# A mixer block on one NeuronCore: all of x and w2 first, w3 and w4 issued by ScalarE behind early gelus, layer 1 nearly in one piece, its later tiles turned by DMA

## The chip, the cores and the metric

The kernel runs on one core of a Trainium2 chip. The metric is the device time of one execution in microseconds (us). Several executions of each kernel are taken in rounds beside the kernel before on the same chip; the profiled execution is one of them. A run counts as slow when it is over 1.5% above the fastest of its kernel.

## The reference

```python
B, S, D, F = 1, 2048, 512, 1792          # bf16
def reference(x, w1, w2, w3, w4):
    h = gelu(layernorm(x) @ w1)          # layer 1
    # four quarters of h's columns are shifted along S by +1, -1, +2, -2 (zeros come in)
    x1 = x + shifted(h) @ w2             # "mixing"
    return x1 + gelu(layernorm(x1) @ w3) @ w4   # "up2" and "down"
```

S is cut into 16 tiles of 128 rows. A normalized tile must be transposed ("turned") before it can enter a product. A turn is made either by TensorE (four 128x128 matmuls against the identity into PSUM, then a copy by ScalarE or DVE) or by a DMA transpose from SBUF to SBUF, issued by SyncE.

## The kernel before

The program is a list of operations with what they read and write. TensorE's order is written out in SCRIPT; loads are listed in LOADS, and an operation goes to SyncE's queue unless "@act" sends it to ScalarE's. The order on the other engines is found by a list scheduler with fixed costs. "tyN" or "tpN" in SCRIPT turns tile N on TensorE (N over 15 means tile N-16 of layer 2), "up1:g" is layer 1's product of group g, "mix:t" the mixing of tile t, "up2:g" and "down:t" are layer 2. Every tile not turned in SCRIPT is turned by DMA:

```python
GROUPS = {1: (1, 1, 1, 1, 2, 1, 4, 2, 2, 1), 2: (2, 4, 4, 2, 4)}     # tiles in a group
LOADS = """
x1 x2 tp2 x0@act w1a w1b x3 x4-5 tp5 w2a w2b x6-7 w3 tp17 w4a x8-10 w4b tp6 x11-12 tp1 tp16 x13-15
"""
SCRIPT = """
warm:9 sa:0 sb:0 ty:1 ra:0 rb:0 ty:2 up1:1 th:0 up1:2 mix:0 ty:3 ty:5 mix:1 ty:4 up1:3-4 ty:16 mix:2 ty:17
mix:3 up2:0 mix:4 up1:5 down:1 down:0 mix:5 up1:6-7 mix:8 mix:6 up1:9 mix:9-10 up1:8 mix:7 mix:11 up2:1
...   # (cut)
"""

def load(item):
    name, _, eng = item.partition("@")
    eng = eng or "sp"
    ...   # (cut) one dma_start of whole x tiles, or of a half ("a", "b") or all of a weight

def ln(layer, t):
    ...   # (cut) statistics on DVE or ScalarE, rstd by pow on GpSimd, normalization into xn_buf
    if q not in pe_tp:
        pg.add("sp", f"tp{q}",
               lambda e: e.dma_start(xT[:, :, P * t : P * (t + 1)], xn_buf[:, slot(q), :], transpose=True),
               reads=[(("xn", slot(q), hh), q) for hh in (0, 1)],
               writes=[(("xT", t, c), layer) for c in range(DC)], queue="tp")
```

SyncE's queue carries loads, DMA turns and, later, outputs, in order. Before, w3 and w4 stand in that same queue between loads of x.

## Time and profile before

| what | value |
|---|---|
| time, median of the first three runs | 135.79 us (135.78 to 136.6) |
| time beside the experiments, medians | 135.15 to 135.44 us |
| span of the profiled run | 134.6 us (its time was 135.96 us) |
| layer 2's first product starts | 16.8 us |
| turns on TensorE / by DMA | 9 (one of them of h) / 24 |

The chain of waits, read in order of time, names for every moment what the end of the program was waiting for; as long as it names TensorE alone, nothing can be gained by removing a wait elsewhere. The prediction shows these lines. The DMA turns as the view of the transposed tile lists them, smallest, median and largest time from issue to landing:

```profile
DMA to landing us min/median/max: 2.4/2.5/5.9
```

A turn takes 2.5 us when nothing else moves; the ones that took up to 5.9 us stood behind loads in the same queue.

### The profile page before, as it was taken

The page shows a single profiled execution, that of the slowest core. Times are in us where ns is not written, and L with a number is a line of the kernel's source. Part 1 is how long each engine was busy: PE and PEld are TensorE (multiplying, and loading weights), DVE is VectorE, ACT ScalarE, POOL GpSimd, SP SyncE. Part 2 cuts the span into 40 slices and gives each one's busy share as a digit, 9 for nine tenths or more (in the row PEclk, how much of TensorE's full clock was granted, in tenths as well). Part 3 has the DMA queues.
Part 4 walks back from the last instruction along what each step waited for, and adds up shares of the span by engine and source line. Part 5 has one row for each costly group of instructions (what it writes and reads, how often), then busy time and mean ns, then how long its engine had stood idle before and what let it go on. Part 6 is the DMA issues. An engine that isn't in the chain of part 4 may idle for free.

```text
span 134.6 us, 2001 instructions
## 1 busy us (share of the span) xinstructions
PE 130.9 (97%) x776; PEld 71.5 (53%) x789; DVE 50.8 (38%) x134; ACT 58.4 (43%) x92; POOL 29.7 (22%) x68
## 2 busy tenths in 40 slices
PE   8799999999999999999999999999999999999994
PEld 3287688544656444478544444444444444444464
DVE  2689996856178930070061004232222200012222
ACT  5779349989544275547315554000000155520000
POOL 2444549892102860006010001200000000000000
DMA  5999998445452134100411000211111100001112
GB/s 136 323 345 399 361 304 234 90 81 105 90 115 85 24 75 98 39 0 0 83 39 39 0 0 0 65 52 44 39 39 53 64 0 0 0 5 39 39 39 78
DMA packets 21289, 12.19 MB, mean 91 GB/s; under 512 B 13856, under 2 KB 20768, under 8 KB 21280
## 3 DMA queue, kind: packets, MB, share of 16 engines
q1 hardware_dynamic: 20704, 11.80, 32.7%
q10 hardware_dynamic: 576, 0.26, 0.7%
q8 instruction: 6, 0.10, 0.3%
q14 instruction: 3, 0.02, 0.1%
HBM read 6.82 MB, written 2.10 MB: 66 GB/s over the span
## 4 chain that ended last, share of the span: by engine, by line
PE 93%; DMA 4%; SPq 1%; issue 1%; DVE 0%
PE y_ps L626 46%; PE o_ps L695 36%; PE o_ps L666 10%; DMA w_sb<-in_w_dram 4%; PE y_ps L490 1%; SPq L368 1%; PE y_ps L528 0%; SPq L377 0%; DVE o_sb L703 0%; PE o_ps L594 0%; SPq L857 0%
## 5 line engine op out<-in xcount | busy, mean ns | idle before, releaser
L626 PE MATMUL y_ps<-xnT,w_sb 128*128 128x512 bf16 (+2 forms) x421 | 63.4, 308 | 0.2
L626 PEld LDWEIGHTS y_ps<-xnT,w_sb 128*128 128x128 bf16 x424 | 38.3, 98 | 24.8
L641 ACT ACTIVATE h2T<-y_ps 128x1024 bf16<-128x1024 f32 (+1 forms) x29 | 28.6, 993 | 48.8 <-PE y_ps L626 48.6
L695 PE MATMUL o_ps<-w_sb,h2T 128*128 128x512 bf16 (+3 forms) x247 | 48.6, 355 | 0.3
L695 PEld LDWEIGHTS o_ps<-w_sb,h2T 128*128 128x128 bf16 x252 | 23.5, 98 | 24.7
L703 DVE TENSOR_TENSOR o_sb<-o_ps,x_sb 128x512 bf16<-128x512 f32 (+3 forms) x18 | 11.4, 632 | 47.1 <-PE o_ps L695 47.1
L423 POOL TENSOR_TENSOR rstd<-mv,neghalf 128x1 f32<-128x1 f32 x21 | 11.5, 549 | 23.6 <-DVE mv L418 14.8
L416 DVE BATCH_NORM_STATS2 st<-x_sb 128x6 f32<-128x512 bf16 x21 | 14.1, 678 | 3.4 <-DMA x_sb<-in_x_dram 3.2
L666 PE MATMUL o_ps<-w_sb,hT 128*128 128x512 bf16 x59 | 14.9, 379 | 0.3
L423 POOL TENSOR_TENSOR rstd<-vpe,neghalf 128x1 f32<-128x1 f32 x11 | 6.0, 547 | 29.4 <-DVE vpe L412 29.3
L673 DVE SCALAR_TENSOR_TENSOR x_sb<-o_ps,x_sb 128x512 bf16<-128x512 f32 x5 | 3.4, 686 | 19.2 <-PE o_ps L666 19.2
L641 ACT ACTIVATE hT<-y_ps 128x512 bf16<-128x512 f32 (+1 forms) x10 | 8.1, 807 | 5.5 <-PE y_ps L626 5.3
L677 DVE TENSOR_TENSOR x_sb<-o_ps,x_sb 128x512 bf16<-128x512 f32 x11 | 7.6, 687 | 4.4 <-PE o_ps L666 4.1
L666 PEld LDWEIGHTS o_ps<-w_sb,hT 128*128 128x128 bf16 x64 | 6.0, 98 | 5.7
L457 POOL TENSOR_SCALAR xn_buf<-x_sb,rstd,nmr 128x512 bf16<-128x512 bf16 x11 | 8.4, 765 | 0.8 <-DVE nmr L450 0.4
L400 ACT ACTIVATE junk<-x_sb 128x512 bf16<-128x512 bf16 x11 | 6.9, 624 | 2.2 <-DVE x_sb L673 2.2
L454 ACT ACTIVATE xn_buf<-x_sb,nmr,rstd 128x512 bf16<-128x512 bf16 x8 | 6.3, 806 | 0.6 <-POOL nmr L450 0.6
L445 DVE TENSOR_SCALAR xn_buf<-x_sb,mv,rstd 128x512 bf16<-128x512 bf16 x12 | 5.3, 442 | 2.8 <-POOL rstd L423 2.6
L720 PE MATMUL o_ps<-zeros 128*128 128x512 bf16 x9 | 4.0, 631 | 0.4 <-DVE zeros L347 0.4
L395 ACT ACTIVATE junk<-x_sb 128x512 bf16<-128x512 bf16 x6 | 3.7, 624 | 0.8 <-DMA x_sb<-in_x_dram 0.8
L418 DVE BATCH_NORM_AGGREGATE mv<-st 128x2 f32<-128x9 f32 x21 | 3.8, 189 | 0.3
L450 POOL TENSOR_SCALAR nmr<-mv,rstd 128x1 f32<-128x1 f32 x13 | 3.4, 263 | 0.7
(34 smaller groups left out, 28.6 us busy)
## 6 DMA issues: line engine op xcount, KB each, us to landing
out_dram<-o_sb SPq DMA_DIRECT2D x15, 128.0 KB, 1.7
w_sb<-in_w_dram SPq DMA_DIRECT2D x1, 1792.0 KB, 9.7
w_sb<-in_w_dram SPq DMA_DIRECT2D x2, 896.0 KB, 11.5
w_sb<-in_w_dram SPq DMA_DIRECT2D x4, 256.0 KB, 5.2
x_sb<-in_x_dram SPq DMA_DIRECT2D x3, 256.0 KB, 5.1
x_sb<-in_x_dram SPq DMA_DIRECT2D x2, 384.0 KB, 8.9
x_sb<-in_x_dram SPq DMA_DIRECT2D x3, 128.0 KB, 2.6
xnT<-xn_buf SPq DMA_TRANSPOSE x24, 2.5
```

The source lines that it names most:

```text
L400: (lambda d: (lambda e: e.activation(d, src, ACT_F.Square, accum_out=sums[:, q, 1:2])))(junk[:, b, :]),
L416: pg.add("dve", f"bnst{q}", lambda e: e.bn_stats(st9[:, q, 0:6], src), reads=rs, writes=[(("st", q), 0)], dur=605)
L423: lambda e: e.tensor_tensor(col(rstd), var, neghalf[:], ALU.pow),
L445: lambda e: e.tensor_scalar(dst, src, mv[:, q, 0:1], rstd[:, q : q + 1], ALU.subtract, ALU.mult),
L454: f = lambda e: e.activation(dst, src, ACT_F.Identity, bias=nmr[:, q : q + 1], scale=rstd[:, q : q + 1])
L457: f = lambda e: e.tensor_scalar(dst, src, rstd[:, q : q + 1], nmr[:, q : q + 1], ALU.mult, ALU.add)
L626: ins = e.matmul(y_ps[:, p, W * i : W * (i + 1)], wsb[:, dc, P * fc : P * (fc + 1)], src[:, dc, P * t0 : P * t0 + W], start=(dc == 0), sto ...
L641: (lambda d, s: (lambda e: e.activation(d, s, ACT_F.Gelu_apprx_tanh)))(dst, ysrc),
L666: ins = e.matmul(dst, hT[:, j, c0 : c0 + P], w2_sb[:, j, :], start=(j == 0), stop=(j == DC - 1))
L677: f = lambda e: e.tensor_tensor(x1_sb[:, t, :], dst, x_sb[:, t, :], ALU.add)
L695: ins = e.matmul(dst, h2T[:, fc, P * t : P * (t + 1)], w4_sb[:, fc, cs], start=(fc == 0), stop=(fc == FC - 1))
L703: (lambda d, c: (lambda e: e.tensor_tensor(o_sb[:, oi, c], d, x1_sb[:, t, c], ALU.add)))(dst, cs),
```

## The change

The intent: less work on TensorE, the bounding engine (fewer turns, wider groups in layer 2), w3 and w4 out of the way of x, and layer 1 nearly in one piece. TensorE's script and the assignments of side work were searched anew. The diff, cut (constants of the scheduler's cost model, further assignment tables and a list of small priority offsets are left out):

```diff
+        for a, b in self.gates:            # order on one engine without a semaphore
+            assert named[a].eng == named[b].eng, (a, b)
+            order_only.add((named[a].idx, named[b].idx))
 ...
-GROUPS = {1: (1, 1, 1, 1, 2, 1, 4, 2, 2, 1), 2: (2, 4, 4, 2, 4)}
+GROUPS = {1: (1, 2, 1, 1, 1, 2, 1, 2, 2, 2, 1), 2: (4, 4, 4, 4)}
 ...
 LOADS = """
-x1 x2 tp2 x0@act w1a w1b x3 x4-5 tp5 w2a w2b x6-7 w3 tp17 w4a x8-10 w4b tp6 x11-12 tp1 tp16 x13-15
+x0-1 x2 x3 w1a x5 w1b x4 w3@act>gelu1_3_0 tp4 x6 x7 x8 w2a tp4 w2b x11 x9-10 tp3 x15 x12-13 x14
+w4@act>gelu1_1_0
 """
 SCRIPT = """
-warm:9 sa:0 sb:0 ty:1 ra:0 rb:0 ty:2 up1:1 th:0 up1:2 mix:0 ty:3 ty:5 mix:1 ty:4 up1:3-4 ty:16 mix:2 ty:17
-mix:3 up2:0 mix:4 up1:5 down:1 down:0 mix:5 up1:6-7 mix:8 ...
+warm:10 sa:0 sb:0 ty:2 ty:1 ra:0 rb:0 ty:3 up1:1 ty:5 th:0 up1:2 ty:4 up1:4 mix:0 up1:3 mix:1 mix:4 up1:5
+mix:3 mix:2 up1:6 mix:5-6 up1:7 mix:7 up1:8 mix:9 mix:8 up1:9 mix:11 mix:10 up1:10 mix:13 mix:12 up2:1 ...
 """
 ...
-            eng = eng or "sp"
+            eng = eng.partition(">")[0] or "sp"
```

"w3@act>gelu1_3_0" reads: issue w3 from ScalarE after it has issued the gelu of group 3 (tile 4).

## The prediction

> **What bounds the kernel now.** I read the page's busy times first, then the chain of work that ended last in order of time, then the start of the timeline, then the waits.
>
> ```profile
> PE 130.9 (97%) x776; PEld 71.5 (53%) x789; DVE 50.8 (38%) x134; ACT 58.4 (43%) x92; POOL 29.7 (22%) x68
> PE   8799999999999999999999999999999999999994
> PE 93%; DMA 4%; SPq 1%; issue 1%; DVE 0%
> ```
>
> TensorE is busy in 97% of the span, and the slices show no hole after the first two; the other engines have room on average. A busy TensorE could still be waiting in small pieces, so the chain in order of time decides:
>
> ```profile
> 1.47 5.13 DMA w_sb<-in_w_dram
> 6.61 0.05 issue
> 6.65 0.61 PE y_ps L528 x2
> ...
> 8.60 0.92 PE y_ps L626 x16
> ...
> 16.83 6.11 PE y_ps L626 x56
> ...
> 36.81 1.73 PE o_ps L666 x8
> ...
> 129.36 3.48 PE o_ps L695 x43
> 132.84 0.02 issue
> 132.87 0.26 DVE o_sb L703
> ```
>
> Columns: start, length, what. From 6.65 us, where the second half of tile 0's first product starts, to 132.84 us the chain is TensorE alone, with pieces of 0.05 us of issue. It gives me rates: 128 columns 0.92/16, other pieces 0.89/16, so 0.0556 us; 256 columns 6.11/56 = 0.1091; 512 columns 1.73/8 = 0.2158. By these I count what the program must run after 6.65: 460 matmuls of 512 columns (64 mixing, 16 for the group of four tiles in layer 1, 168 in the three large groups of layer 2, 210 down, 2 of tile 0) are 99.27 us; 174 of 256 columns (48 layer 1, 112 layer 2, 14 tail) 18.98; 80 of 128 columns 4.45; 28 transposes (seven tiles) 1.57; the tail's 160 and 96 columns about 1.6. Sum 125.87. The stretch lasts 126.19. So only 0.3 us of it is waiting: no rearrangement can gain by removing waits after the start. After the last matmul come 1.76 us to the end of the span (134.6 - 132.84), and the time is 1.19 us over the span (135.79 - 134.6).
>
> The start is set by loads:
>
> ```profile
> 5.95 1.31 PE L528 MATMUL y_ps<-w_sb,xnT 128*128 128x512 bf16 x4 [0.74 <-DMA w_sb<-in_w_dram]
> 6.07 3.59 SPq L368 DMA_DIRECT2D x_sb<-in_x_dram  x1
> 6.93 0.70 DVE L416 BATCH_NORM_STATS2 st<-x_sb 128x6 f32<-128x512 bf16 x1 [0.76 <-DMA x_sb<-in_x_dram]
> ```
>
> The first row begins when the first half of w1 lands (5.95); its second pair of matmuls waits for the second half (6.65). The second row is a load of x issued with w3 and w4 queued ahead on SyncE's queue: SyncE was held 3.59 us, where a small load ordinarily takes about 0.45.
>
> **What the Trainium skill says.** "TensorE: Matmul & The Clock Gate", section "Wait — 56ns, not 53.3ns?", gives start to start N / 2.4 GHz plus about 2.5 ns per matmul; the rates above agree (55.6 and 215.8 ns), so wider groups gain only 2.5 ns per matmul saved. "DMA: Bandwidth & Descriptors", section "Issuing engines are not separate DMA queues", says that DMAs of all issuing engines run on the same 16 engines and interleave, and that a second issuer saves only sequencer time. The trace before has one x load on ScalarE beside SyncE's at 0.2 us, neither lengthened, too small to test sharing. "Perfetto Trace Analysis", section "DMA Instruction — HWDGE (DVE, Sync)", says the profiled issue lasts until the descriptors are generated, and that generation can outrun the descriptor buffer; the 3.59 us above agrees with a full buffer. This is the danger in putting 1.8 MB loads on ScalarE. No run here shows yet how SyncE's transposes fare beside another queue's load.
>
> **The change part by part.**
>
> (1) Transposes. Tiles 16 and 17 (layer 2) no longer turn on TensorE, and tiles 1 and 2 both turn before the first product, inside the wait for w1. After the second half of tile 0's product four turns remain (tiles 3, 5, 4 and the turn of tile 0's h) in place of seven: 12 x 0.056 = -0.67 us on the bounding engine.
>
> (2) Groups. Layer 2 goes from 2,4,4,2,4 tiles to four fours: 112 matmuls of 256 columns (12.22) become 56 of 512 (12.08), -0.14 us. Layer 1 splits its group of four into twos: 16 x 0.2158 = 3.45 becomes 32 x 0.1091 = 3.49, +0.04 us. Together -0.10. With (1), TensorE's work after the start falls by about 0.77 us. There is nothing else to take: the columns of the two layers, the mixing and the down product are unchanged.
>
> (3) Load order. Before, x1, x2, x0 and half of w1 (640 KB), then the other half (896 KB in all) come first. After, x0-1, x2, x3 stand before the first half (768 KB at its end) and x5 before the second (1152 KB). Before, the second half landed 0.70 us after the first: 256 KB in 0.70 us, 370 KB per us. So the first half lands about 0.35 later (6.3) and the second 256/370 = 0.7 later (7.35). The start moves by +0.7 us. In that wait the turns of tiles 1 and 2 fit: each needs statistics 0.69, aggregate 0.19, the power on GpSimd 0.55, and a normalization of 0.41 (DVE) or 0.76 (GpSimd), so from x at about 3 us both are ready near 6. The tenth warm matmul lies in the same wait and costs nothing.
>
> (4) Layer 1 runs almost without a break. By the rates, after a start at 7.4 the fifteen other tiles and twelve mixings end at about 34 us, where before up2 and down pieces stretched this to about 80 us. By about 25 us DVE must have done the statistics of ten tiles or so (0.69 + 0.19), nine normalizations (0.41), and five or six residual adds (0.69): 8.8 + 3.7 + 3.8 = 16.3 us in spans, and a little less as they overlap at their ends, of some 18 us available. Before, DVE was busy 4.77 and 4.59 us of 5 in the two windows from 10 to 20 us, so such a density is reached but leaves little.
>
> (5) w3 and w4 on ScalarE, behind the gelu of tile 4, about 15 us. Before, w3 and half of w4 took SyncE 1.52 us together, the other half 1.83 us. I estimate 1.5 to 3.5 us of ScalarE. After that gelu TensorE has two mixings, the product of tiles 6-7, two more mixings and the product of tile 8 before a mixing needs the next gelu: 4 x 0.86 + 1.75 + 0.89 = 6.1 us, less the gelu before (0.6) and the next (1.0). So up to about 4 us is hidden. The weights, 3.67 MB at 0.37 MB/us, need 10 us, arrive near 26 us, and layer 2 starts at 34: not on the path.
>
> (6) Transposes by DMA of tiles 8 to 15 now fly with that load. Before, transposes issued between 16 and 24 us, with loads in the queue, landed after 4.5 to 5.9 us; the median is 2.5. Tile 8 is due at about 19 us, 9-10 at 22, 11-12 at 24. Here a delay of 2 us would reach TensorE in part.
>
> Sum: 135.79 - 0.77 + 0.70 = 135.7 without new waits; I put +0.1 for the middle of (4) to (6), whose likely result is nothing but whose unlikely ones are large: **135.8 us**.
>
> **Rivals.** First, new stalls in layer 1: the load on ScalarE's queue delays SyncE's transposes, or ScalarE is held longer than 4 us by its own issue. For it: 4.5 to 5.9 us landings and the 3.59 us of SyncE above. Against: in the old order these transposes sat behind loads in the same queue, which the new one avoids, and all x is issued before. It would make 137 to 140. Second, the start is not later: the early transfer is limited by latency rather than bytes (the memory rate was only about 150 KB per us between 2.5 and 3.5 us before), so w1 lands as before. The full -0.77 then shows, and 135.0 results. Third, DVE becomes the bound of the dense layer 1: its windows were already 92 to 95% busy. Because it catches up only when TensorE waits, that would cost 0.5 to 2 us, 136.3 to 137.7. Fourth, a gain over 2% would need 2.7 us; with 125 us of columns after the start this would require starting 2 us earlier than now, which the later w1 excludes.
>
> **Range and chances.** The lower end is the work saving with no later start and a tighter stretch: 134.8. The upper end gives the stall rivals 2 us: 137.8. Slower by over 2% (beyond 138.5) needs nearly 3 us of stall; I give it 0.12. Faster by over 2%: 0.01.
>
> **What would show each step.** In the chain after, the first product's second half starts at 7.2 to 7.5 (step 3), TensorE alone follows for about 125.4 us (steps 1, 2), with no DMA or DVE piece. The count of turns on TensorE through y_ps falls from 32 to 24. ScalarE's two weight issues sum to 1.5 to 3.5 us, and the product of layer 2 starts near 34 us. The prediction is wrong if the chain between 15 and 30 us goes through DMA transposes, DVE or ScalarE for more than 1 us, if the start is before 6.9, or if a matmul's rate changes.

## The result

The changed kernel takes 142.85 us (median of 4 runs, 142.26 to 144.81) against 135.78 for the kernel before. The ratio of the fast runs is 1.050 (95% interval 1.041 to 1.059): it is slower, and far outside the predicted range. Ratios in this document are the mean time of one kernel's fast runs over that of the other's of the same rounds, so not quite the ratio of the medians quoted. The four runs had granted TensorE clocks of 0.976 (144.81 and 143.42 us) and 0.988 (142.29 and 142.26 us); the kernel before always showed 1.000. The profiled run was the one of 144.81 us, counted as slow.

The page of the changed kernel (busy times; TensorE's busy slices; its granted clock in the same slices; shares of the chain that ended last):

```profile
PE 135.4 (94%) x742; PEld 69.4 (48%) x742; DVE 48.7 (34%) x139; ACT 58.9 (41%) x91; POOL 27.0 (19%) x59
PE   8799980999999999999999999999999999999992
PEclk9999997589999999999999999999999999999999
PE 84%; DMA 8%; DVE 5%; POOL 0%; issue 0%; DVEq 0%; SPq 0%
```

TensorE's share fell from 97 to 94%, a hole stands in the seventh slice, and right behind it the granted clock falls to half. "Busy" rose from 130.9 to 135.4 us although there is less work, mainly since slow matmuls are busy longer. The chain in order of time (start, length, what) shows where the end was set:

```profile
6.37 1.03 PE y_ps L497 x8
7.41 1.71 PE y_ps L535 x4
...
15.93 9.03 DMA xnT<-xn_buf
24.96 0.05 issue
25.01 1.89 PE y_ps L633 x16
26.89 3.38 PE o_ps L673 x8
30.27 1.75 PE y_ps L633 x16
```

The piece of 9.03 us is the DMA turn of tile 8. It was issued at 15.93 us and landed at 24.96; TensorE had nothing to do for the last 4.07 us of it. TensorE's timeline names the wait in brackets (before the bracket: start, length, what), and the view of the transposed tile shows how late turns landed at most:

```profile
25.01 1.89 PE L633 MATMUL y_ps<-xnT,w_sb 128*128 128x128 bf16 x16 [4.07 <-DMA xnT<-xn_buf]
DMA to landing us min/median/max: 2.4/2.5/11.2
```

Then 16 matmuls of 128 columns took 1.89 us (0.89 before), and 8 of 512 columns 3.38 us (1.73): half clock until about 30 us.

The difference of the two profiled runs, 143.5 - 134.6 = 8.9 us of span, adds up as follows. Tile 0's first product ends at 9.11 us (7.41 + 1.71) in place of 7.26 (6.65 + 0.61): +1.85. The gap: +4.07. Half clock behind it: (1.89 - 0.89) + (3.38 - 1.73) = +2.65. Less work on TensorE: -0.77 by the prediction's count. From the last matmul to the end of the span 2.5 us in place of 1.76: +0.8. Together 8.6; 0.3 us stays unassigned. This profile is the slowest of the four runs. Its first product ran at half rate (four matmuls in 1.71 us), which the profile of e_w4late, a fast run 7.6 us slower than the kernel before, did not share; the gap and the half clock behind it did not need that.

The DMA view of two stretches of the changed kernel shows what the turn was waiting for (q10 is ScalarE's queue, q1 SyncE's; packets, MB, share of the 16 engines' time; then turns issued in the stretch and their median us to landing). First 17 to 20 us:

```profile
q10 hardware_dynamic: 240, 0.86, 90.9%
...
xnT<-xn_buf SPq DMA_TRANSPOSE x3, 9.8
```

Then 24 to 26 us:

```profile
q10 hardware_dynamic: 535, 0.55, 82.8%
q1 hardware_dynamic: 534, 0.13, 31.5%
```

From 17 to 20 us SyncE's queue moved no packet at all (q1 is not listed): 240 rows of w3, 3.5 KB each, went by, while turns that had been issued stood still. From 24 to 26 us, with w4's rows of 1 KB, the two queues moved 535 and 534 packets: one for one. A turn has some 577 packets (13,856 packets under 512 B for 24 turns before), so at 267 per us it needs 2.2 us; alone, turns pass at 500 and more per us (e_bothlate). The Trainium skill, "DMA: Bandwidth & Descriptors", section "Queues, rings and completion order", says that each engine goes round robin between queues packet by packet; the second stretch agrees. The section does not describe the first.

ScalarE itself was not held up: its two weight issues took 0.44 and 0.57 us in the timeline. SyncE was: its issue of the turn at 18.71 us took 3.20 us (median 1.27).

### The profile page after: what moved, and what is told of

The parts are those of the page before. It is cut to its first block, busy times and chain, and to the rows that moved or that the text cites. A ratio compares the mean times of both kernels' runs of the same rounds, so it can differ in the third digit from the quotient of the medians.

```text
span 143.5 us, 1924 instructions
## 1 busy us (share of the span) xinstructions
PE 135.4 (94%) x742; PEld 69.4 (48%) x742; DVE 48.7 (34%) x139; ACT 58.9 (41%) x91; POOL 27.0 (19%) x59
## 4 chain that ended last, share of the span: by engine, by line
PE 84%; DMA 8%; DVE 5%; POOL 0%; issue 0%; DVEq 0%; SPq 0%
PE y_ps L633 41%; PE o_ps L702 34%; PE o_ps L673 8%; DMA xnT<-xn_buf 6%; DMA x_sb<-in_x_dram 2%; DVE st L423 2%; PE y_ps L535 1%; PE y_ps L497 1%; DVE xn_buf L452 1%; DVE mv L425 0%; DVE x_sb L680 0%; POOL rstd L430 0%; DVE xnT L505 0%; DVE nmr L457 0%; DVE o_sb L710 0%
## 5 line engine op out<-in xcount | busy, mean ns | idle before, releaser
L633 PE MATMUL y_ps<-xnT,w_sb 128*128 128x512 bf16 (+2 forms) x384 | 64.7, 328 | 4.1 <-DMA xnT<-xn_buf 4.1
L633 PEld LDWEIGHTS y_ps<-xnT,w_sb 128*128 128x128 bf16 x384 | 35.3, 100 | 33.6 <-DMA xnT<-xn_buf 4.6
L648 ACT ACTIVATE h2T<-y_ps 128x1024 bf16<-128x1024 f32 x28 | 28.7, 1024 | 22.0 <-PE y_ps L633 22.0
L673 PE MATMUL o_ps<-w_sb,hT 128*128 128x512 bf16 x64 | 17.1, 410 | 0.0
L648 ACT ACTIVATE hT<-y_ps 128x1024 bf16<-128x1024 f32 (+1 forms) x10 | 8.0, 812 | 9.4 <-PE y_ps L633 9.4
L464 POOL TENSOR_SCALAR xn_buf<-x_sb,rstd,nmr 128x512 bf16<-128x512 bf16 x9 | 6.9, 772 | 8.5 <-DVE nmr L457 7.8
L684 DVE TENSOR_TENSOR x_sb<-o_ps,x_sb 128x512 bf16<-128x512 f32 x9 | 6.2, 689 | 6.3 <-PE o_ps L673 6.1
L452 DVE TENSOR_SCALAR xn_buf<-x_sb,mv,rstd 128x512 bf16<-128x512 bf16 x15 | 6.9, 462 | 1.0 <-POOL rstd L430 0.8
L680 DVE SCALAR_TENSOR_TENSOR x_sb<-o_ps,x_sb 128x512 bf16<-128x512 f32 x7 | 4.8, 684 | 6.1 <-PE o_ps L673 6.1
L497 PE MATMUL y_ps<-ident,xn_buf 128*128 128x128 bf16 x24 | 3.1, 281 | 1.1 <-DVE xn_buf L452 1.1
```

Of the source, the lines that this page charges most:

```text
L452: lambda e: e.tensor_scalar(dst, src, mv[:, q, 0:1], rstd[:, q : q + 1], ALU.subtract, ALU.mult),
L464: f = lambda e: e.tensor_scalar(dst, src, rstd[:, q : q + 1], nmr[:, q : q + 1], ALU.mult, ALU.add)
L633: ins = e.matmul(y_ps[:, p, W * i : W * (i + 1)], wsb[:, dc, P * fc : P * (fc + 1)], src[:, dc, P * t0 : P * t0 + W], start=(dc == 0), sto ...
L648: (lambda d, s: (lambda e: e.activation(d, s, ACT_F.Gelu_apprx_tanh)))(dst, ysrc),
L673: ins = e.matmul(dst, hT[:, j, c0 : c0 + P], w2_sb[:, j, :], start=(j == 0), stop=(j == DC - 1))
L684: f = lambda e: e.tensor_tensor(x1_sb[:, t, :], dst, x_sb[:, t, :], ALU.add)
```

## The experiments

Fourteen kernels ran. In all but four (e_turn8, e_turn6, e_turn6rows, e_pieces) every other instruction kept the changed kernel's order on its engine; but for e_swap this was done by moving finished operations in the list after the scheduler had run. "move(a, b)" puts a right behind b; "fill" puts matmuls on zeros into TensorE's order.

**e_swap: which weight comes first**

```diff
-... x4 w3@act>gelu1_3_0 ...
-w4@act>gelu1_1_0
+... x4 w4@act>gelu1_3_0 ...
+w3@act>gelu1_1_0
```

> Changed kernel with w4 issued first on ScalarE and w3 second; all other instructions in the changed kernel's order. In the changed kernel SyncE's queue moved no transpose packets from 17 to 20 us and then one packet for each packet of the weight queue (250 against 250 per us beside w4's 1 KB rows). Theory A, sharing by packet behind a batch already fetched: w4's rows are 3.5 times smaller, so the batch passes in about 1 us, transposes then move 250 packets per us, tile 8's lands near 20 us, the gap falls from 4.1 to under 1 us and the time to 137.5 to 139.5. Theory B, descriptor generation: SyncE's transposes get no descriptors while ScalarE's two loads are being written, in either order: still no packets for 3 us or more, gap 3 us or more, time 141.5 to 144.5.

Measured: 144.96 us (143.65 to 148.01), ratio 1.072. Theory A missed: between 16 and 19 us only 15 packets of SyncE's queue moved beside 925 rows of w4. After that it was one for one in each us (285 against 281 from 21 to 22, 109 against 107 from 24 to 25 with w3). So the shut-out (the time in which turns get next to no packets) of about 3 us does not depend on which weight is first; in rows it was about 60 per engine here and about 20 in the changed kernel, in bytes about 1 MB both times. The time lies near theory B's figure, but the next run speaks against B's reason. Three of the four runs had 0.988 and 143.65 us, 0.976 and 146.03, 0.965 and 148.01, which looks as if the time went with the granted clock; the fourth, 0.976 and 143.89, does not fit.

**e_w4late: only w3 at the old place**

```diff
+        move("dma_w4", "gelu2_1_0")
```

> Changed kernel with only w4's issue moved later on ScalarE, behind the second gelu of the first group of layer 2; w3 stays where it was. Theory B (generation): w3's 512 rows fit into the buffer, so SyncE's transposes get descriptors at once; packets of both queues run from 17 us on, one for one at about 100 per us while w3 runs, tile 8's 576 packets need 5.5 us, it lands near 22.5, the gap is 1 to 2 us, later tiles go at full rate after 22; time 138.5 to 140.5. Theory A (a fetched batch): 17 to 20 us is as empty as before, tile 8 lands at 23 to 24, gap 2.5 to 3.5; time 140 to 141.5.

Measured: 142.71 us (142.28 to 143.81), ratio 1.057; neither theory's number. The chain shows why both missed:

```profile
12.38 7.54 DMA xnT<-xn_buf
19.92 0.14 issue
20.06 3.57 PE y_ps L633 x16
```

The gap (4.2 us) stands one product earlier, before tiles 6 and 7, whose turn was issued at 12.4 us and landed at 19.9. In this run the first product ran at full clock and everything came 1.4 us earlier, so the weight issue caught tile 7's turn and not tile 8's. SyncE's queue moved no packet from 16 to 18 us. With w4 out of the way, w3 alone does that. Theory B (turns wait until both loads' descriptors are written) falls; theory A's batch stays possible in a weaker form: about 1 MB of a load that has just begun passes ahead of turns.

**e_fillgap: keep TensorE busy in the gap**

```diff
+        fill(18, "up1_6_0", "mix3")     # before tile 8's product
```

> Changed kernel with 18 matmuls on zeros put into TensorE's 4.07 us gap before tile 8's product; nothing else moves. Theory: after the gap TensorE ran at half clock from 25 to 30 us, which cost some 2.65 us beside the gap itself. With TensorE kept busy the clock stays and only the gap is left: the matmuls after 25 us run at full rate at once, time 2 to 3 us below the changed kernel, 139.5 to 140.8. Rival: the slow stretch has another cause (reads of SBUF contending with the loads): no change, 142 to 144.5.

Measured: 144.77 us (143.02 to 146.28), ratio 1.062. A miss in design: the gap stood at tile 7 again (20.90 us), so the 18 matmuls (3.98 us at 25.88) were pure extra work. The run tells nothing of its question. It was tried again as e_fill7.

**e_turn8: tiles 8 to 12 on TensorE**

```diff
-mix:3 mix:2 up1:6 mix:5-6 up1:7 mix:7 up1:8
+mix:3 ty:8 mix:2 up1:6 ty:9 mix:5 ty:10 mix:6 up1:7 ty:11 mix:7 ty:12 up1:8
```

> Changed kernel with tiles 8 to 12 of layer 1 turned on TensorE (20 turns more, 1.1 us of TensorE) instead of by DMA; the loads stay as in the changed kernel, other engines' order is searched anew. Theory: the gap is the late DMA turn of tile 8 alone, so gap and slow clock (6.7 us together) vanish, less 1.1 us of turns and perhaps 0.5 to 1.5 us of waits for tiles 13 to 15, whose DMA turns still compete with the load: 137 to 139. Rival: DVE and ScalarE cannot feed the dense layer 1 either, so gaps of 2 us or more stay: 139.5 or more.

Measured: 139.41 us (138.45, 138.89, 139.92 at clock 1.00; the profiled run 145.28 at 0.976), ratio 1.029. In the profile, which is the slow run, the gap before tiles 6 and 7 is still there (4.3 us), and no DMA turn of tiles 8 to 12 comes behind it. No trace shows the gap of the three fast runs. They are some 3 us faster than the changed kernel at the price of 1.1 us of TensorE; since the other engines' order was searched anew, that the five turns fewer brought this is not shown.

**e_turn6: all of layer 1 on TensorE**

```diff
-mix:4 up1:5 mix:3 mix:2 up1:6 mix:5-6 up1:7 ...
+mix:4 ty:6-7 up1:5 mix:3 ty:8 mix:2 up1:6 ty:9 mix:5 ty:10 mix:6 up1:7 ty:11 mix:7 ty:12 up1:8 ... ty:15 mix:10 up1:10
```

> Changed kernel with all of layer 1's tiles turned on TensorE (tiles 6 to 15 too, 40 turns more, 2.2 us); the loads and their issue on ScalarE stay; other engines' order is searched anew. Four runs have shown that the changed kernel's gap can also stand at tile 7 (16 to 20 us), so this asks whether any DMA turn in layer 1 is needed for the loss. Theory (load shuts out the DMA turns, and the half-clock windows only follow the gap): no gap over 1 us before 30 us, granted clock 1.00, time 135.3 - 0.77 + 2.2 + 1.0 to 1.85 for the later start = 137.7 to 138.6, up to 139.2 if the DMA turns of layer 2's first tiles still collide. Rival (DVE and ScalarE cannot feed the dense layer 1): gaps of 2 us or more in all, clock below 1.00, time 139.5 to 142.

Measured: 141.92 us (141.82 to 141.97, all at clock 1.00), ratio 1.049: the rival's time. Whom TensorE waited for (us in total, times, longest):

```profile
PE y_ps L633 <- DVE mv L415: 1.1, 1, 1.1
PE y_ps L633 <- ACT xn_buf L461: 0.9, 1, 0.9
PE y_ps L633 <- DVE xnT L505: 0.9, 1, 0.9
PE y_ps L497 <- DVE xn_buf L452: 0.9, 1, 0.9
```

No DMA turn of layer 1 and no half clock is left, but now DVE and ScalarE are late: ten more tiles must be copied out of PSUM, in an order searched anew. So this run removes the gap and puts another bound in its place; it does not show that the changed order itself starves TensorE, since its own order never ran here.

**e_turn6rows: the same with tile 0's product first**

```diff
-warm:10 sa:0 sb:0 ty:2 ty:1 ra:0 rb:0
+warm:10 sa:0 sb:0 ra:0 rb:0 ty:2 ty:1
```

> The kernel of e_turn6 with, in addition, tile 0's first product put before the turns of tiles 2 and 1 on TensorE, as in the kernel before. In the changed kernel's trace w1 had landed by 6.5 us, yet the product ended only at 7.7 (or 9.1 at half clock), because it stood behind turns that waited for DVE. Theory: the product's end moves back to about 7 us and the time falls by 0.5 to 1 us against e_turn6. Rival (the later loads of w1 set the start, as predicted): no change within 0.3 us.

Measured: 142.30 us (142.18 to 142.41), 0.4 above e_turn6. Neither: with the new order of ScalarE the gelu of tile 0 came ahead of the copies of tiles 1 and 2, and the first wide product started at 8.9 us, not 7.9. Confounded; tried again as e_now3rows.

**e_bothlate: both weights later**

```diff
+        move("dma_w3", "gelu1_8_0")
+        move("dma_w4", "gelu2_1_0")
```

> Changed kernel with both weight loads moved later on ScalarE: w3 behind the gelu of tiles 11-12, w4 behind the second gelu of layer 2; all other instructions in the changed kernel's order. Theory: no load is in flight at 16 us, tiles 6 to 12 are turned in 2.5 to 4 us each and the gap at tile 7 or 8 is gone with its half-clock windows (saving 6 to 7 us of the changed kernel's); w3 then arrives near 31 us and shuts out the turns issued from 25 us on for about 3 us, which can cost 0 to 3 us once. Time 136.3 to 139.5. Rival (DVE and ScalarE bound the dense layer 1): gap stays between 14 and 22 us, 141 or more.

Measured: 139.19 us (138.29 to 139.96), ratio 1.029, clock 0.998 to 1.00. This is the cleanest run: all orders on all engines are the changed kernel's, only the two issues moved. Its chain:

```profile
15.75 1.89 PE y_ps L633 x16
17.64 1.73 PE o_ps L673 x8
...
31.49 4.89 DMA xnT<-xn_buf
36.37 0.14 issue
36.51 12.25 PE y_ps L633 x56
```

From tile 0's turns until the chain turns to the DMA at 31.5 us it is TensorE without a hole. The DMA view from 17 to 20 us, where the changed kernel's queue stood still:

```profile
q1 hardware_dynamic: 1386, 0.34, 56.5%
...
xnT<-xn_buf SPq DMA_TRANSPOSE x3, 2.5
```

Turns land after 2.5 us in place of 9.8. The rival (DVE and ScalarE bound the dense layer 1) is refuted. And the same thing shows where w3 now flies: it was issued at 26.4 us, SyncE's queue moved no packet from 31 to 32 us, and layer 2's first turns were late by 2.3 us of TensorE's time.

**e_pieces: w3 in quarters on SyncE, other orders searched anew**

```diff
+x0-1 x2 x3 w1a x5 w1b x4 x6 x7 x8 w2a w2b x11 x9-10 x15 x12-13 x14 tp6 tp7 tp8 w3p tp9 w3q tp10 w3r tp11 w3s tp12
+w4@act>gelu2_1_0
```

> Changed kernel with w3 issued by SyncE in four quarters, one between each two of its DMA turns of tiles 8 to 12, and w4 behind layer 2's second gelu on ScalarE; TensorE's order unchanged, others searched anew. One queue serves in order, so a turn waits for at most a quarter (0.46 MB, 1.25 us). Theory (the loss is one large load of another queue in front of the turns): turns of tiles 6 to 8 land in 2.5 to 4 us, those of 9 to 12 in 4 to 5, gaps in layer 1 below 2 us in all; 136 to 139. Rival (any load in flight beside the turns costs the same): gaps of 4 us or more with half-clock windows, 140 or more.

Measured: 142.56 us (141.38 to 143.65), ratio 1.051. Inconclusive: TensorE waited 4.4 us, in two waits that end at 6.3 and 12.9 us, for normalizations by DVE ahead of early turns, before the first piece of w3 was issued (14.7 us), because the new order put other work first; half clock followed here too.

**e_fill7: the fill at the right place**

```diff
+        fill(18, "up1_5_0", "mix1")     # before the product of tiles 6 and 7
```

> The fill tried again at the right place: four of the runs so far had the gap at tile 7's turn (15.8 to 20 us), so 18 matmuls on zeros (3.9 us) stand before the product of tiles 6 and 7 in the changed kernel's order; nothing else moves. Theory: the half clock after the gap is a consequence of TensorE's idleness and costs 1.7 us for each half-clock window beside the gap itself; kept busy, TensorE stays at full clock, the profile's granted clock is 1.00 throughout, and the time falls to 138.8 to 140.8. Rival (the slow matmuls come from the load's traffic): the matmuls after the fill are slow all the same and the time stays at 142 to 144.5.

Measured: 141.93 us (141.43 to 141.98), ratio 1.049, clock 1.00 in all four. The profile's granted clock in 40 slices:

```profile
PEclk9999999999999999999999999999999999999999
```

The clock stayed up and the spread of the times fell to 0.55 us where the changed kernel's was 2.5: so the half clock follows from TensorE's idleness. But the time fell by less than 1 us, not by 2 to 4. After the fill the chain goes through the queue again (a turn from 22.11 to 30.51 us), with 1.8 us of TensorE idle in two waits. In this stretch the turns set the pace until the loads are through; a TensorE at half clock merely waits less. Gap and half clock may therefore not be added up as if either could be saved alone.

**e_quarter: one quarter of w3 at the old place**

```diff
+        # four DMAs of w3, one chunk each, in place of one
+        for k, anchor in enumerate(["gelu1_3_0", "gelu1_8_0", "dma_w31", "dma_w32"]): quarter(k, "act", anchor)
+        move("dma_w4", "gelu2_1_0")
```

> As e_bothlate, but one quarter of w3 (0.46 MB, 1.25 us of transfer) stands at the changed kernel's place behind the gelu of tile 4; the other quarters come behind the gelu of tiles 11-12, w4 behind layer 2's second gelu. Theory A (the turns behind a load are shut out until about 1 MB of it, or all of it, has passed): the gap at tile 7 is there but is 0.5 to 2 us in place of 4.2; time 136.5 to 139.5. Theory B (a new load of another queue shuts the turns out for a fixed 3 us, whatever its size): gap 3 us or more, with a half-clock window, 140 or more.

Measured: 142.10 us median of 139.12 (clock 1.00), 142.04 and 142.17 (0.988) and 145.0 (0.976). Only one run counts as fast, but the profile answers: while the quarter's 128 packets passed, turns moved none from 15 to 16 us and 140 from 16 to 17; they moved 945 in the next us. Tile 7's turn still landed late:

```profile
12.35 5.86 DMA xnT<-xn_buf
18.22 0.14 issue
18.35 3.46 PE y_ps L633 x16
```

TensorE waited 2.6 us for it, with half clock behind it (16 matmuls of 256 columns in 3.46 us), and 1.8 us before layer 2, behind the three quarters issued together: between theory A's 0.5 to 2 us and theory B's 3. What speaks against a fixed 3 us are the packets: the shut-out ends with the load when the load is short. Each step of 0.012 in the mean clock went with some 3 us here.

**e_spaced: quarters, spaced on ScalarE**

```diff
+        for k, anchor in enumerate(["gelu1_5_0", "gelu1_6_0", "gelu1_7_0", "gelu1_8_0"]): quarter(k, "act", anchor)
+        move("dma_w4", "gelu2_1_0")
```

> w3 in quarters on ScalarE, behind the gelus of tiles 6-7, 8, 9-10 and 11-12, some 2 to 4 us apart; w4 behind layer 2's second gelu; all else in the changed kernel's order. A try at a version that keeps the dense layer 1 without the shut-out. If each quarter holds the turns back by 1.3 us at most: gaps of 0 to 1.5 us in all, w3 complete near 30 us, layer 2 starts at 31.5 to 33; time 135.0 to 137.0. If each quarter shuts them out for 3 us: 138.5 or more.

Measured: 140.57 us median of 136.84 (clock 1.00) and 140.51, 140.62, 140.69 (0.988): the best single run with correct results and all weights beside the turns, and 3.9 us worse in the profiled run. The granted clock of that run:

```profile
PEclk9959999999999999999999999999999999999999
```

Its one half-clock window lies at the start (third slice; 6.56 to 9.97 us in the trace's clock record), where the first product ran at half rate. The longest wait, 2.5 us from 26.34 us, did not bring one. So not all of the 3.9 us can be put down to the loads.

**e_sppieces: the same quarters on SyncE**

```diff
+        for k, anchor in enumerate(["tp8", "tp9", "tp10", "tp11"]): quarter(k, "sp", anchor)
+        move("dma_w4", "gelu2_1_0")
```

> w3 in the same quarters, but issued by SyncE behind its turns of tiles 8, 9, 10 and 11, so that one queue serves loads and turns in order; w4 behind layer 2's second gelu on ScalarE; all else in the changed kernel's order (the earlier try with pieces on SyncE had a new order on DVE, and lost its time there). If sharing between queues is what hurts: each turn waits at most one quarter, gaps 0 to 2 us, 135.3 to 137.5. If it makes no difference which queue: as e_spaced within 0.7 us.

Measured: 139.61 us (139.37 to 139.64 at clock 1.00; 141.69 at 0.988), ratio 1.032. Neither: in-order service in one queue costs as well, since turns stand behind quarters (landing 5 to 6 us from 18 to 23 us). The two placements differ in time too, so they don't compare queue with queue alone; but a loss does not need a second queue.

**e_now3: no w3 at all (wrong)**

```diff
+        pg.seq.pop(at("dma_w3"))
+        move("dma_w4", "gelu2_1_0")
-            wsb, wn, src = (w1_sb, "w1", xnT) if layer == 1 else (w3_sb, "w3", xnT)
+            wsb, wn, src = (w1_sb, "w1", xnT)      # columns taken modulo w1's width
```

> Wrong result on purpose: w3 is never loaded, layer 2's first product reads w1's columns in its place (same shapes and counts); w4 comes behind layer 2's second gelu; all else in the changed kernel's order. Theory (the loss is the weight loads in front of the turns): with no load before 36 us there is no gap, granted clock 1.00, and the time is the old one less the work saved plus the later start: 135.2 - 0.77 + 0.4 to 0.7 = 134.8 to 135.5. Rival (the dense order itself costs, DVE and ScalarE): 136.5 or more, with gaps before TensorE's products in layer 1 or at layer 2's start.

Measured: 136.57 us (median of 6, 135.82 to 136.84), ratio 1.009 (1.006 to 1.013), result wrong. In the profile of the 135.82 us run these are all of TensorE's waits for another engine:

```profile
PE y_ps L497 <- DVE xn_buf L452: 0.9, 1, 0.9
PE o_ps L727 <- DVE zeros L353: 0.4, 1, 0.4
```

The first is the turns of tiles 2 and 1 at the start, the second lies before the first warm matmul; no DMA stands among them, and the last matmul ends at 132.50 us (before: 132.84). Without the load the gap, the half clock and the later stall are all gone: about 6.3 of the changed kernel's 7.1 us. The time is still 1.1 us above what was expected and 1.2 above the kernel before: it is the rival's number (136.5 or more) without the rival's gaps. The profiled run does not show the reason, as it was the fastest of the six. w4 delayed turns here too: issued at 35.8 us, it made those issued from 35.2 to 40.1 us land after 5.3 to 9.3 us, and TensorE did not wait for any of them.

**e_now3rows: what sets the start**

```diff
+        for n in ("rows0_1", "rows0_0"): move(n, "ev0_1")    # tile 0's product before the turns of tiles 2 and 1
```

> The kernel of e_now3 (wrong on purpose) with tile 0's first product before the turns of tiles 2 and 1, all else in the same order. Theory (the turns that wait for DVE set the start, not w1): the product ends near 7.0 in place of 7.7 and the turns follow, so TensorE does 0.86 us of work inside the wait; time 0.3 to 0.8 us lower, 134.2 to 135.0. Rival (w1's landing sets it, as predicted): within 0.2 us of e_now3.

Measured: 136.72 us (136.48 to 137.4), ratio 1.010, within 0.2 of e_now3. TensorE's timeline in this run:

```profile
6.47 0.61 PE L535 MATMUL y_ps<-w_sb,xnT 128*128 128x512 bf16 x2 [0.58 <-DMA w_sb<-in_w_dram]
6.91 0.61 PE L497 MATMUL y_ps<-ident,xn_buf 128*128 128x128 bf16 x8
8.07 0.38 PE L497 MATMUL y_ps<-ident,xn_buf 128*128 128x128 bf16 x4 [0.56 <-ACT xnT L505]
```

The second half of w1 lands at 6.4 us, not at the predicted 7.35. The product then ends at 7.1 us, but the turns come behind it, TensorE waits 0.56 us for their copies, and the first wide product starts at 8.5 us where e_now3 started it at 7.9. The wait moved and grew. The time fits the rival's number, not its reason: w1's landing and the tiles' readiness (6.16 us in e_now3) lie within 0.3 us of each other, and either order pays for both.

## Why the prediction was wrong

**What bounds the kernel, the counts of step 1 and 2: right.** TensorE ran for 124.86 us from the end of tile 0's product (7.64) to the last matmul (132.50) in e_now3, and the sum of the prediction, less that product's second half, is 124.7. The turns through y_ps fell from 32 to 24 matmuls. The rates did not change at full clock. (Two slips without effect: the profiled run took 135.96 us, so the time is 1.36 us over its span, not 1.19; and the load of x that held SyncE for 3.59 us had w3 and only half of w4 ahead of it.) What was left to win, 0.77 us, was as small as said; that a gain over 2% was as good as excluded was right.

**Step 3, the start: right in size only.** Predicted +0.7 through w1's landing at 7.35. In the 11 experiments' profiles with the changed order at full clock the product ended near 7.7, +0.4; the wait that ends last is that of the turns for DVE, not w1, which lands at 6.4. That the number came near is luck. By the second rival w1 would land as before, and so it did: at 6.50 us in the changed kernel's profile against 6.61, with 1152 KB in place of 896 up to its end; but its 135.0 did not show, as the start moved all the same. In the changed kernel's own profile and in e_spaced's these first products ran at half rate (1.71 us for four). For e_spaced the clock record has 0.50 there; that of the changed kernel has no entry before 9.63 us, and the views read 1.00 until then.

**Step 4, the dense layer 1: right.** e_bothlate ran the same order with TensorE without a hole to 34.16 us, where the wait for a turn begins. The third rival falls with it. Layer 2 started at 34.0 us in e_now3, as predicted (34); the SCRIPT has fourteen mixings before it, not the twelve that the prediction names, with which its rates give about 32.

**Step 5, ScalarE's own cost: too high, without effect.** 0.44 + 0.57 = 1.0 us measured against 1.5 to 3.5. What held SyncE for 3.59 us before did not hold ScalarE.

**Step 6 failed, and with it the sum.** "Here a delay of 2 us would reach TensorE in part" was the term that had to be sized, and "+0.1 for the middle of (4) to (6)" is what it got. The delay was 6 to 9 us: landings of 8.4 to 11.2 us for the five turns issued from 15.9 to 23.7 us, where the prediction read 4.5 to 5.9 off the kernel before (4.3 to 5.9 by the trace). Of this 4.1 us reached TensorE directly. The prediction's own sign of being wrong, a chain that goes through DMA turns for more than 1 us between 15 and 30 us, is the piece of 9.03 us. The first rival named this very mechanism, but the argument against it, that the new order avoids having turns behind loads in one queue, was wrong: in another queue the load got ahead all the same. Moving the two issues alone took 3.7 us away (e_bothlate), leaving w3 out 6.3 (e_now3).

**A term was left out.** An idle TensorE lost its clock. The Trainium skill, "TensorE: Matmul & The Clock Gate", section "What's actually happening", says that an idle window of about 3.4 us brings the array to half clock and that the window runs freely. The trace agrees with the window, not with so long an idleness. The entries of the trace's clock record, 9.63, 23.29 and 30.11 us, lie four and two times 3.41 us apart, and the clock was 0.50 for the last two of these windows. But TensorE was idle only from 20.94 us, so for 2.35 of the 3.41 us before the clock fell, and in e_w4late for 1.95. In seven profiles the clock fell in or just behind gaps of 2.55 (e_quarter) to 5.09 us (e_fillgap); gaps of 2.35 (e_bothlate) and 2.51 us (e_spaced) left it at 1.00; only the half clock at the start of e_spaced came behind shorter waits (0.3 and 1.3 us). A half-clock window of 3.4 us costs 1.7 us of work if TensorE is busy in it, which is 0.012 of 141 us, and nearly all mean clocks come in these steps (1.000, 0.988, 0.976, 0.965). The first rival's "137 to 140" lacks this term; but it is not the whole of what that range missed, since e_fill7 kept the clock and still took 141.93 us. The changed kernel's runs scatter by 2.5 us and e_fill7's by 0.55, so part of the scatter goes with the half clock (e_bothlate scatters by 1.7 us without it). That each run's gap caught a different number of windows is likely and not shown: one of the four runs was traced, and in e_w4late the times did not follow the mean clocks (142.53 us at 0.988, 142.28 at 0.976).

**What stays open.** Why a load that has begun shuts out the turns of the other queue for about 1 MB was not settled: not the order of descriptor generation for both loads (e_w4late), not the row size (e_swap), not a fixed time (e_quarter). The whole of w3 on SyncE's queue at the same place, which would help to tell the queue from the load, was not tried. Nor was the 1.2 us by which e_now3 stays above the kernel before, although its profiled run shows no gap; a first product at half rate in the other runs would do it, but no trace of those runs exists. No kernel here beat the one before: with 0.77 us to win, the best correct run of a changed order, 136.84, loses it again at the weights.

## What to carry to other kernels

A time per transfer read off a quiet or differently queued stretch does not hold once a large load is put beside it: look at how many packets of each queue pass in each microsecond, and place bulk loads where no small transfer is due (moving two issues, and nothing else, took 3.7 us off here, and w4 in e_now3 delayed turns that nobody waited for). When an engine has 0.3 us of slack in 126, weigh a change by what it can start to hold up, not by the work it saves. And expect half clock behind a TensorE gap of more than 2.5 us (it followed in seven profiles of seven), but don't add the two blindly: while something else sets the pace, a slower TensorE merely waits less.

## What the Trainium skill lacked or had wrong

- "DMA: Bandwidth & Descriptors", section "Queues, rings and completion order": round robin by packet was seen (535 against 534 packets), but not that a load just begun on ScalarE's queue leaves SyncE's DMA transposes without any packet first: none from 17 to 20 us in the changed kernel, 15 beside 925 from 16 to 19 us in e_swap, none from 16 to 18 us in e_w4late.
- The same page, section "Rules for kernel authors", says that a transpose next to ordinary DMAs needs nothing. The row is about wrong results, and in that it holds (all were correct where all weights were loaded). It does not hold for time: landing went from 2.5 us to between 8.4 and 11.2 us.
- "Perfetto Trace Analysis", section "DMA Instruction — HWDGE (DVE, Sync)": the issue of a DMA of 1,792 rows returned at 16.7 us, after 0.57 us, although 512 rows of 3.5 KB had been issued right ahead and moved until about 23 us; no sign of the full buffer that it draws was met on ScalarE.
- "TensorE: Matmul & The Clock Gate", section "What's actually happening", asks for an idle window of about 3.4 us; here the clock fell after 2.35 us of idleness (changed kernel) and after 1.95 (e_w4late).
- No page says that a clock record can begin late: in the changed kernel its first entry is at 9.63 us, and until then the views read 1.00 while matmuls of 512 columns take 427 ns (4 in 1.71 us at 7.4 us).
